# A gated mix of a causal convolution and a spectral filter on one core: chunk 4's products summed on VectorE and POOL, chunk 2's kv unfolded, gate weights loaded apart, halves, and a new order

## The chip, the core and the metric

The kernel runs on one core of a Trainium2 chip. The core has a matrix engine (TensorE, PE in the profile, with PEld for its weight loads), a vector engine (VectorE, DVE), an engine for activations and scaled copies (ScalarE, ACT), a general engine (GpSimd, POOL) and a queue that only issues transfers (SyncE, SP). Matmul results land in PSUM, which this kernel uses as eight banks of 128 x 512 floats; everything else lies in SBUF. POOL reads and writes SBUF only. Transfers are issued from SP and POOL and run on 16 DMA engines.

The metric is the device time of one execution in microseconds, as a median over runs.

## What is computed

Two branches over 2048 positions and 640 channels, mixed by a gate. All data are 32-bit floats.

```python
g = sigmoid((A_q * gate_w).sum(-1, keepdims=True))
# branch A: short causal convolution of k (4 taps), times v, then a causal
# convolution over all 2048 positions, plus a skip term, times q
kv = k_shift * v
y  = irfft(rfft(pad(kv)) * rfft(pad(ssm_k)))[:S] + kv * ssm_D
a  = q * y
# branch B: a two-dimensional real FFT, a product with complex weights, and back
b  = irfft2(rfft2(x) * (w_r + 1j * w_i))          # x is A_q
out = g * a + (1 - g) * b
```

## The kernel before

Both branches are done with Fourier transforms written as matmuls with constant matrices. The length 2048 is split into 64 x 32 and a twist in between; the 640 channels are five chunks of 128. What would be a complex product is four real products, of which pairs are added or subtracted.

Branch B works on one large tile XX. `fwd(u)`, for u from 0 to 7, loads a piece of the transposed input (`xT`), makes four sums and differences of 640 elements on VectorE or POOL (two of a first stage, two of a second) and transforms over the channels (L309, and L316 for the remaining rows) with the matrix `df`. Four columns of `df` hold the gate's weights, so that the gate's sums fall out of the same matmuls; `gate_cols` computes these columns from `gwx`, which lies behind `df` in the same load. `b1(u)` does the first step over the positions (ten times), `bs2(i)` the second and the product with the spectral weights (eight times, with two products and a sum for each of the real and imaginary parts), `i1(u)` the first step back (six times). `bu(n)` is the last step over the positions (16 times), and `dic(v)` the transform back over channels, for v from 0 to 7: matmuls (L447, L453), four scaled copies on ACT (L461), two sums (L465), two more sums (L467), and the store of the rows.

Branch A works chunk by chunk (c from 0 to 4) on one of three slots of a tile YY. `kv(u)`, two for each chunk, does the short convolution as matmuls (L486), the product with v on VectorE (L489), a sum and a difference of the halves, the fold (L495), and a transpose (L498). `hf(u)` loads the long filter. `s1` is the first transform (L530, twice as many matmuls where kv was not folded) and two transposes out of PSUM (L540). `s2(c, m)`, four steps for each chunk, is the second transform of both kv and filter (L560), a copy of the filter's half to SBUF by ACT (L565) and the two products (L581 and L578). For the chunks in `PESUM` the products are written back into YY, and the inverse transform `is1a` adds and subtracts them by having four groups of matmuls accumulate where it would else have two. For the others the products go to two M buffers, and two sums (L586) on VectorE or POOL write YY. `is1a` transforms (L271) and transposes back out of PSUM (L276). `afin(c, n0)`, two for each chunk, is the last transform (L622) and the product with q and the gate (L628). I number afin 0 to 9 (2c for n0 = 0, 2c + 1 for n0 = 8), is1 likewise by chunk and half.

The two branches meet in the output in memory. For chunks 0 to 2 branch A stores first and the rows of `dic` are added to it by an accumulating transfer from POOL (L471). For chunks 3 and 4 `dic` stores its rows (L474) and `afin` follows: afin 6 and 8 by an accumulating transfer from POOL (L641), afin 7 and 9 (those in `BACK`) by reading the rows back (L637), adding them on VectorE (L638) and storing the sum (L639). These read-backs wait until the stores of the four `dic` of their half have landed.

Each unit of work is recorded as an operation with its engine, and nothing runs in the order of the code: `_emit` goes through the list `ORDER`, the result of a planner, which gives the order in which the operations are issued to the in-order queues of all engines. `ON_DVE` says which of the sums and products that either engine could do lie on VectorE; the others lie on POOL. `SLOTS` gives each buffer its place: there are five V buffers (128 x 1024), three T, four M, two L, two H, one G (for k), and the PSUM banks. Where an operation waits follows from what it reads and writes. With `GATE`, an operation of POOL waits for the last VectorE operation ahead of it in the order that reads its operands from SBUF.

## Time and profile before

| | us |
|---|---|
| median of three runs | 285.04 |
| lowest and highest | 282.61 and 285.54 |
| the profiled execution | 283.68 |
| its span, from first to last instruction | 281.6 |

TensorE's mean granted clock in the profiled execution was 0.984 of full speed.

In the rows of the profile a group of instructions is told by its line, its engine and the tiles that it writes and reads. The rows of fp32 matmuls count two records for each matmul of the code. "Idle before" is the time in which the engine had nothing to do in front of these instructions, with what ended it. The chain is the work that ended last, followed back from the end.

### The profile page before, as it was taken

The numbers are of one execution on the slowest core, as the hardware profiler recorded it, in microseconds if no ns is written. First come the engines' busy times: TensorE is split into PE (matmuls) and PEld (weight loads), VectorE is DVE, ScalarE is ACT, GpSimd is POOL, SyncE is SP. The second block draws the span as 40 slices with busy tenths as digits, with TensorE's granted clock in tenths as the row PEclk, the third lists the DMA queues.
The fourth block names the chain that finished last, engine by engine and source line by source line (L and its number), as shares of the span: only waits on it lengthen the run. The fifth ranks groups of instructions, "written<-read, shape, count | busy, mean of one in ns | idle before, by whom it ended". The sixth has DMA issues, their size and how long they took to land.

```text
span 281.6 us, 10200 instructions
## 1 busy us (share of the span) xinstructions
PE 246.3 (87%) x4562; PEld 144.9 (51%) x4562; DVE 224.1 (80%) x250; ACT 103.6 (37%) x232; POOL 150.1 (53%) x116
## 2 busy tenths in 40 slices
PE   0798789899999999788998988999999999999950
PEld 0674445554334454125445433667776677776450
DVE  3979489759998999999999999896464895664970
ACT  1052404451233333362263030546644374445500
POOL 0047557535005574798989710079888328339420
PEclk9999979999999999999999999999999999999996
DMA  7999979959996255687269963626548538737789
GB/s 277 421 416 346 330 264 420 410 123 365 278 389 230 70 98 199 188 338 254 82 165 352 260 121 99 276 80 231 146 115 139 131 54 149 228 54 97 134 200 211
DMA packets 28251, 61.53 MB, mean 218 GB/s; under 512 B 1712, under 2 KB 18480, under 8 KB 26544
## 3 DMA queue, kind: packets, MB, share of 16 engines
q1 hardware_dynamic: 22512, 51.45, 49.8%
q0 software_dynamic: 5696, 9.44, 21.9%
q8 instruction: 36, 0.59, 0.8%
q14 instruction: 7, 0.06, 0.1%
HBM read 50.39 MB, written 10.49 MB: 216 GB/s over the span
## 4 chain that ended last, share of the span: by engine, by line
PE 64%; DVE 15%; DMA 8%; POOL 5%; issue 4%; SPq 1%; ACT 1%; DVEq 0%; POOLq 0%; ACTq 0%
PE banks L560 11%; PE banks L271 11%; PE banks L356 7%; PE banks L447 7%; PE banks L420 7%; PE banks L530 5%; PE banks L622 5%; DMA XX<-xT 4%; DMA V<-h 4%; DVE YY L540 3%; DVE XX L276 3%; PE banks L309 3%; PE banks L453 2%; PE banks L486 2%; PE banks L428 2%
## 5 line engine op out<-in xcount | busy, mean ns | idle before, releaser
L540 DVE STREAM_TRANSPOSE YY<-banks 128x1024 f32<-128x1024 f32 x40 | 48.2, 1227 | 8.4 <-PE banks L530 8.4
L560 PE MATMUL banks<-YY,s2a 64*32 64x256 f32 x1280 | 43.0, 389 | 2.7 <-issue 1.6
L565 ACT ACTIVATE H<-banks 128x512 f32<-128x512 f32 x40 | 23.5, 598 | 39.9 <-PE banks L560 20.2
L495 POOL TENSOR_TENSOR T<-V 128x512 f32<-128x512 f32 x12 | 15.8, 1330 | 41.8 <-DVE V L489 22.0
L560 PEld LDWEIGHTS banks<-YY,s2a 64*32 64x32 f32 x1280 | 24.0, 105 | 19.7 <-issue 6.7
L271 PE MATMUL banks<-YY,ca 32*64 32x512 f32 x512 | 31.1, 607 | 0.6 <-DVE YY L540 0.4
L309 PE MATMUL banks<-cc,XX 128*64 128x162 f32 (+1 forms) x256 | 22.1, 330 | 8.7 <-DVE cc L287 8.7
L612 ACT ACTIVATE V<-V,g 128x128 f32<-128x128 f32 x72 | 21.9, 394 | 14.4 <-DMA V<-q 14.4
L309 PEld LDWEIGHTS banks<-cc,XX 128*64 128x64 f32 x256 | 19.4, 150 | 14.2 <-DVE cc L287 8.7
L581 DVE TENSOR_TENSOR YY<-banks,H 128x512 f32<-128x512 f32 x24 | 16.3, 682 | 13.1 <-ACT H L565 12.8
L276 DVE STREAM_TRANSPOSE YY<-banks 128x2048 f32<-128x2048 f32 x10 | 23.1, 2313 | 3.3 <-PE banks L271 2.9
L303 POOL TENSOR_TENSOR XX<-M 128x640 f32<-128x640 f32 x8 | 12.4, 1557 | 19.3 <-DVE XX L303 13.7
L461 ACT ACTIVATE M<-banks,om 128x320 f32<-128x320 f32 x32 | 14.2, 528 | 21.9 <-PE banks L453 16.2
L395 POOL TENSOR_TENSOR XX<-M,M 128x642 f32<-128x642 f32 x15 | 19.7, 1328 | 4.1 <-DVE M L389 3.4
L271 PEld LDWEIGHTS banks<-YY,ca 32*64 32x64 f32 x512 | 13.3, 129 | 15.5 <-issue 10.6
L356 PE MATMUL banks<-XX,cb 128*128 128x512 f32 (+1 forms) x42 | 20.9, 632 | 0.0
L622 PEld LDWEIGHTS banks<-YY,is2a 128*64 128x64 f32 x320 | 18.1, 134 | 5.3 <-DVE YY L540 1.9
L622 PE MATMUL banks<-YY,is2a 128*64 128x128 f32 x320 | 20.3, 279 | 0.5 <-DVE YY L276 0.5
L447 PEld LDWEIGHTS banks<-di,L 128*128 128x128 f32 x128 | 17.6, 190 | 5.5 <-ACT L L436 3.0
L586 POOL TENSOR_TENSOR YY<-M,M 128x512 f32<-128x512 f32 x14 | 18.5, 1355 | 3.4 <-DVE M L578 1.1
L420 PE MATMUL banks<-cc,XX 128*128 128x128 f32 x128 | 19.4, 295 | 0.4 <-DVE M L578 0.4
L447 PE MATMUL banks<-di,L 128*128 128x160 f32 x128 | 19.5, 306 | 0.0
(70 smaller groups left out, 417.3 us busy)
## 6 DMA issues: line engine op xcount, KB each, us to landing
G<-k SPq DMA_DIRECT2D x10, 1024.0 KB, 8.3
L<-w SPq DMA_DIRECT2D x8, 642.0 KB, 4.7
XX<-xT SPq DMA_DIRECT2D x8, 640.0 KB, 8.7
V<-v SPq DMA_DIRECT2D x10, 512.0 KB, 6.7
V<-h SPq DMA_DIRECT2D x10, 512.0 KB, 9.0
V<-h POOLq DMA_DIRECT2D x10, 512.0 KB, 8.0
V<-q SPq DMA_DIRECT2D x10, 512.0 KB, 5.6
out_dram<-V SPq DMA_DIRECT2D x8, 512.0 KB, 4.6
```

The lines of the kernel that those rows point to most:

```text
L271: mm(p[h * 64:h * 64 + 64, j, :nd * 8], is1[r, sg, ri, :], v[r, h * 2 + src, :, d0:d0 + nd, :].rearrange("p m d e -> p d m e"), start=(i = ...
L276: nc.vector.transpose(by_col(x, d0, nd), p[:, :, :nd * 8].rearrange("p j (d i) -> p d j i", i=8))
L309: mm(bk(p, g_)[ri * 64:ri * 64 + 64, o:o + n], X[:, s, g_ * 64:g_ * 64 + 64], df[:, 0, ri * 323 + o:ri * 323 + o + n], start=(o == 0), sto ...
L356: mm(v(x)[:, e0:e0 + ne], m1b, by_col(XX, d0 + a + e0, ne), start=True, stop=True)
L395: ttop(642, lambda f, ri=ri, o=o, dst=dst: f(dst(), T(t1)[:, ri], T(t2)[:, 1 - ri], op=o), us=1.28, r=[t1, t2, ("t", i, 0, ri), ("t", i, 1 ...
L420: mm(psa[:, t, :, b, :], row(XX, n2)[:, t * 161:t * 161 + 128], W(n2), start=True, stop=True)
L447: mm(bk(p, b)[:, n * 160:n * 160 + 160], U[:, t_, r_], di[:, b * 160:b * 160 + 160], start=(n == 0), stop=False)
L540: op("DVE", dve(1024), lambda b=b: nc.vector.transpose(by_col(YY[:, :, y], a * 64 + b * 32, 32), view(b)), r=[p[b]], w=yk)
L560: mm(ps(p)[j * 32:j * 32 + 32, h].rearrange("p (y r d) -> p y r d", y=2, r=2)[:, :, ri], s2a[r, k, ri * 32:ri * 32 + 32], YY[r, k // 2, y0 ...
L565: op("ACT", act_us(512), lambda p=p, hs=hs: act(sb(hs, 2, 256), ps(p)[:, :, 256:], AF.Copy), r=[p], w=[hs])
L612: act(dst(j), src(j), AF.Copy, scale=g[:, n0 + j:n0 + j + 1])
L622: mm(v()[b * 64:b * 64 + 64, j, :], is2a[:, n2, :], row(YY[:, :, yp], n2), start=True, stop=True)
```

## The change

The diff does these things:

- `PESUM` loses chunk 4. Its products go to two buffers of the pool T (`TP`), two sums for each of the four steps write YY, and its two `is1a` have two groups of matmuls for four.
- `PEFOLD` gains chunk 2: its kv is not folded ahead of the first transform, which has twice as many matmuls there.
- `gwx`, the gate's weights, is loaded into a tile of its own, ahead of `df`, which is now loaded without the four gate columns (in four pieces of 321 columns for each partition). The columns' writers are declared independent of that load.
- The second stage of sums in `fwd` marks each of its halves, and the matmuls are two operations, of which each waits for its half.
- The last adds of afin 7 and 9 and their stores are done in two halves of 512 elements.
- `ON_DVE`, `ORDER` and `SLOTS` are new. Among the things that change place: `fwd(2)` is first where `fwd(0)` was, `fwd(7)` comes behind chunk 0's inverse transforms, afin 4 and 5 stand ahead of `i1`, and is1 7 and afin 6 stand next to the last `dic`, afin 6 behind it.

```diff
 BACK={7,9}
-PESUM={0,2,4}
-PEFOLD=set()
+PESUM={0,2}
+PEFOLD={2}
+TP={4:'T'}
...
+    def apart(these, those):
+
+        for i in these:
+            for j in those:
+                tc.declare_no_dep(i.ins, j.ins.name, reason="the gate's columns are not among the loaded ones")
+
+    def load_df():
+        loaded.append(dma(cc[:, 2048:3340].rearrange("p (b c) -> p b c", c=323)[:, :, 1:322], I["df"].rearrange("p (b c) -> p b c", c=321)))
+        apart(loaded, cols)
+        return loaded[0]
...
-        op("DVE", 0.9, f, w=DF).port = (0, 1)
+        op("DVE", 0.75, f, r=["gwx"], w=["gcol"]).port = (0, 1)
...
-            ttop(640, lambda f, o=o: f(X[:, (2 if o == OP.subtract else 0):][:, :2], Y()[:, 0::2], Y()[:, 1::2], op=o), r=[y], w=[x])
-        blk = ((0, 0, 0, 162), (3, 1, 0, 162), (2, 0, 162, 161), (1, 1, 162, 161))
+            ttop(640, lambda f, o=o: f(X[:, (2 if o == OP.subtract else 0):][:, :2], Y()[:, 0::2], Y()[:, 1::2], op=o),
+                 r=[y, x], w=[("xs", u, int(o == OP.subtract))])
+        blk = ((0, 0, 0, 162), (1, 1, 162, 161), (2, 0, 162, 161), (3, 1, 0, 162))
...
-        op("PE", 2.2, pe, r=[x] + DF, w=p, mode="128x64")
+        for h in range(2):
+            op("PE", 1.1, lambda h=h: pe(h), r=[("xs", u, h), "gcol"] + DF, w=p, mode="128x64")
...
-        t = [] if pesum else [new("M"), new("M")]
+        t = [] if pesum else [new(TP.get(c, "M")), new(TP.get(c, "M"))]
...
-            ttop(1024, lambda f: f(sb(qt, 1024), sb(qt, 1024), sb(bt, 1024), op=OP.add), r=[bt], w=[qt])
-            op("SP", ISS, lambda: dma(out[:, n0:n0 + 8, cs], Q()), r=[qt, bt], kb=524)
+            for h in range(2):
+                hs = slice(h * 512, h * 512 + 512)
+                ttop(512, lambda f, hs=hs: f(sb(qt, 1024)[:, hs], sb(qt, 1024)[:, hs], sb(bt, 1024)[:, hs], op=OP.add), r=[bt, qt], w=[("qh", c, n0, h)])
+                op("SP", ISS, lambda h=h: dma(out[:, n0 + h * 4:n0 + h * 4 + 4, cs], Q()[:, h * 4:h * 4 + 4]), r=[qt, bt, ("qh", c, n0, h)], kb=262)
...
-    op("SP", ISS, lambda: dma(cc[:, 2048:3348], I["df"]), w=DF, kb=666)
+    op("SP", ISS, load_df, w=DF, kb=666)
+    unit("gwx")
+    op("SP", ISS, lambda: dma(gwx, I["gwx"].rearrange("p (a s) -> p a s", a=2)), w=["gwx"], kb=8)
```

The ends of the two orders, by engine, read from the lists (dic 7 is the last transform of the rows; "st1" and "st2" are its first and second pair of sums):

| engine | before | after |
|---|---|---|
| TensorE | bu 14, bu 15, s2 of chunk 4, dic 7, is1 8, is1 9, afin 7, 8, 9 | s2 of chunk 4, bu 14, bu 15, is1 7, dic 7, afin 6, is1 9, is1 8, afin 7, 8, 9 |
| VectorE | products of chunk 4, st1, st1, one st2 of dic 7, transposes of is1 8 and 9, products of afin 7, 8, 9, two adds | products of chunk 4, transpose of is1 7, a sum of chunk 4, product of afin 6, st1, st1 of dic 7, transposes of is1 9 and 8, products of afin 7, 8, 9, four half adds |
| POOL | four sums of dic 6, its accumulating transfer, one st2 of dic 7, its transfer, that of afin 8 | four sums of dic 6, a sum of chunk 4, the transfers of dic 6 and afin 6, both st2 of dic 7, its transfer, that of afin 8 |

29 lines of the change are left out of this document (15 added, 14 removed), and 93 rows, old and new, of tables (ON_DVE, ORDER, SLOTS).

## The prediction

> **What bounds the kernel now.** I read the page first (busy shares, the slices, the shares of the chain that ended last), then the busy time by stretches of 10 us, then the chain in order of time for its end, and the timeline where the chain leaves TensorE.
>
> ```profile
> PE 246.3 (87%) x4562; PEld 144.9 (51%) x4562; DVE 224.1 (80%) x250; ACT 103.6 (37%) x232; POOL 150.1 (53%) x116
> PE   0798789899999999788998988999999999999950
> DVE  3979489759998999999999999896464895664970
> POOL 0047557535005574798989710079888328339420
> PE 64%; DVE 15%; DMA 8%; POOL 5%; issue 4%; SPq 1%; ACT 1%; DVEq 0%; POOLq 0%; ACTq 0%
> ```
>
> ```profile
> 0.00:10.00 10.00, 1.35 (x10) 1.35 (x12) 5.01 (x11) 1.28 (x1) 0.20 (x4) 1.00 0.83 323
> ...
> 20.00:30.00 10.00, 7.99 (x190) 4.42 (x187) 8.35 (x9) 4.11 (x11) 7.58 (x7) 1.00 1.04 354
> 30.00:40.00 10.00, 7.72 (x146) 3.64 (x147) 6.15 (x8) 1.71 (x4) 5.16 (x4) 0.87 0.91 323
> ...
> 110.00:120.00 10.00, 7.77 (x160) 2.25 (x156) 10.00 (x12) 4.62 (x13) 5.99 (x4) 1.00 0.63 194
> 120.00:130.00 10.00, 8.13 (x160) 3.41 (x154) 9.91 (x9) 5.04 (x16) 9.53 (x8) 1.00 0.93 342
> ...
> 240.00:250.00 10.00, 10.00 (x213) 7.57 (x212) 5.47 (x10) 4.61 (x9) 4.31 (x3) 1.00 0.73 189
> ```
>
> Columns: stretch, length, then PE, PEld, DVE, ACT and POOL busy, granted clock, DMA share, GB/s. There are four regimes. Up to 10 us TensorE waits for its first input. From 20 to 40 the DMA share is 0.91 to 1.04 and TensorE is idle 2.01 + 2.28 us. From 110 to 130 VectorE is full (10.00, 9.91) and TensorE is not (7.77, 8.13). From 200 on TensorE is full (the row at 240) and VectorE half idle. Then the end:
>
> ```profile
> 257.14 0.76 PE banks L453 x16
> 257.90 7.37 PE banks L271 x126
> 265.29 2.33 DVE YY L276
> 267.67 3.93 PE banks L622 x56
> 272.76 1.23 DVE V L638
> 274.00 1.23 DVE V L638
> ```
>
> I call the end of the last transform of the rows (L453, at 257.90) the cut. After it come 7.37 us for chunk 4's two inverse groups of four parts, a transpose, 3.93 for two final products, one multiplication and two adds. A second path leaves the same cut:
>
> ```profile
> 258.02 1.78 ACT L461 ACTIVATE M<-banks,om 128x320 f32<-128x320 f32 x4 [2.54 <-PE banks L453]
> 259.89 1.68 DVE L465 TENSOR_TENSOR M<-M 128x640 f32<-128x640 f32 x2 [2.50 <-POOL M L467]
> 262.53 1.56 POOL L467 TENSOR_TENSOR M<-M 128x640 f32<-128x640 f32 x1 [1.89 <-DVE M L467]
> 266.42 1.37 SPq L637 DMA_DIRECT2D V<-out_dram  x2
> 271.54 1.56 POOL L641 DMA_DIRECT2D out_dram<-V  x1 [5.95 <-issue]
> 274.04 2.02 SPq L639 DMA_DIRECT2D out_dram<-V  x2
> V<-out_dram SPq DMA_DIRECT2D x2, 512.0 KB, 6.5
> out_dram<-V SPq DMA_DIRECT2D x2, 512.0 KB, 5.2
> out_dram<-M SPq DMA_DIRECT2D x2, 256.0 KB, 2.2
> ```
>
> The last rows (dic 7) are scaled, added twice and stored, the store lands, and only then are the rows read back that L638 adds. POOL ends at 264.09, the read-backs start at 266.42 and take 6.5 us: 272.9. The path through TensorE reaches its first add at 272.76. **The two paths arrive together**, so shortening one of them alone gives nothing at the end.
>
> **The change, part by part.** I numbered the operations in the order in which the code creates them and read both order lists with that.
>
> ```profile
> L540 DVE STREAM_TRANSPOSE YY<-banks 128x1024 f32<-128x1024 f32 x40 | 48.2, 1227 | 8.4 <-PE banks L530 8.4
> L586 POOL TENSOR_TENSOR YY<-M,M 128x512 f32<-128x512 f32 x14 | 18.5, 1355 | 3.4 <-DVE M L578 1.1 <-ACT M L461 0.9 <-DVE V L511 0.8
> L495 POOL TENSOR_TENSOR T<-V 128x512 f32<-128x512 f32 x12 | 15.8, 1330 | 41.8 <-DVE V L489 22.0 <-PE banks L560 18.1 <-PE banks L530 1.7
> 231.43 1.08 PE banks L530 x32
> 251.29 1.15 PE banks L420 x8
> 252.43 0.36 PE banks L428 x16
> 252.79 1.98 PE banks L560 x58
> 254.77 2.37 PE banks L447 x16
> ```
>
> *Products of chunk 4 not summed on PE.* The two inverse groups go from four parts to two: -7.37/2 = -3.7 us of TensorE, all after the cut. Added are eight sums, four on each of POOL (4 x 1.355 = 5.4 us) and VectorE. They use two T buffers a step, and steps share them, so a step's first product on VectorE now waits for the sums of the step before, and VectorE's later work queues behind it.
>
> *kv of chunk 2 unfolded.* Four folds go (three from POOL, 3 x 1.33 = 4.0 us, one from VectorE) and two first transforms double: +2 x 1.08 = +2.2 us of TensorE.
>
> *Work moved past the cut.* The first final product of chunk 3 (3.93/2 = 1.97 us) now stands behind the cut. TensorE's work before the cut is therefore +2.2 - 2.0, and since the order puts nothing else across it, **+0.2 us**: none of the 3.7 us is saved before the cut.
>
> *After the cut, counted from it.* Before, the first add comes at 272.76 - 257.90 = 14.9 and the span's end at 281.6 - 257.9 = 23.7. In the new order TensorE does afin 6 from 0 to 2.0, is1 9 to 3.9 and is1 8 to 5.7 (1.85 each); VectorE has the multiplication of afin 6 to 3.3 (it waits for TensorE's 2.0), dic 7's two sums to 4.9 (1.68), then two transposes of 2.33 to 9.6. Chunk 4's final products wait for the second and end at 13.5, the last multiplication at 14.7: so of 3.7 us on TensorE only 0.2 come through, since VectorE's queue is late next. The other path: dic 7's last sums are both on POOL (before, one was on VectorE): 4.9 + 2 x 1.56 = 8.0, then 2.3 until the read-backs start as before (264.09 to 266.42): 10.3, and 6.5 to land: 16.8. This path is now 1.9 us later than before. Four half adds of 1.23/2 end at 19.3, not 17.3. Against that, the store is of 256 KB: it takes between 2.2 us (the rows' own store, alone) and 5.2 (the 512 KB store in its crowd). I take 3.2, nearer the small one, since chunk 4's accumulating store (afin 8, from POOL at 12.7) has a lead on the last store of 6.6 us (before, 3.8: 271.5 to 275.3): 19.3 + 0.1 + 3.2 = 22.6, and the 1.1 us between the last landing (275.3 + 5.2 = 280.5) and the span's end make 23.7, as before. I write **0** for the end. The bounds are -3.1 (the read-backs hidden, so that the first add starts at 14.7 and not 16.8, and a store of 2.2 and not 3.2) and +3.2 (below).
>
> *The start.*
>
> ```profile
> 4.89 1.56 DVE L301 TENSOR_TENSOR M<-XX 128x640 f32<-128x640 f32 x2 [4.89 <-DMA XX<-xT]
> 8.51 0.16 DVE L288 TENSOR_TENSOR cc<-gt 128x4 f32<-128x4 f32 x1
> 8.65 4.64 PE L309 MATMUL banks<-cc,XX 128*64 128x162 f32 x32 [8.65 <-DVE cc L287]
> 36.47 1.49 PE L530 MATMUL banks<-V,ca 32*32 32x512 f32 x32 [2.27 <-DVE V L511]
> 42.59 0.69 PE L560 MATMUL banks<-YY,s2a 64*32 64x256 f32 x16
> ```
>
> TensorE starts at 8.65, behind four sums (4.89 to 8.0) and the gate's columns. With the first transform in halves it needs three sums and the columns, which stand second on VectorE: 7.9, so -0.7. The small load of the gate's weights is one more issue (about 0.4 us) ahead of the matrix, hidden behind the 4.89 us that xT takes; uncovered it costs that 0.4. The order also puts one more half transform and its remainder, 1.9 us of TensorE, ahead of the first filter product at 42.59, which otherwise has the same work before it (five whole first transforms and the matmuls of a sixth, three convolutions, four first transforms of chunk 0). One more xT lands ahead: 640 KB at the 323 to 354 GB/s of the rows from 20 to 40 are 1.9 us, and the filter's constants were issued long enough before 42.59 to bear that. If the wait at 36.47 is filled as the list says, the start and this stretch together give **-1.9**; the bounds are 0 and -4.3 (all of the 2.01 + 2.28 idle).
>
> *The middle.* Ahead of the first inverse transform of the spectral half (i1), the new order does 13.6 us more TensorE work (two final products 3.9, four first transforms and two doubled halves 6 x 1.08, two filter products 2.0, one convolution) and 13.7 more on VectorE (eight transposes of 1.227, two multiplications, kv 9, three first sums, less some), but only 1.6 more on POOL, since folds and first sums left it. Both engines' work goes up alike in a stretch where both were nearly full, so i1 starts about 13.6 later and 13.5 less is left behind it: **0**, with bounds of -4.1 (all of TensorE's idle in the rows at 110 and 120, 2.23 + 1.87) and +3.7 (VectorE idles in the added 13.6 us as it does from 20 to 40: 1.65 + 3.85 in 20).
>
> Sum: start and early stretch -1.9, TensorE before the cut +0.2, middle 0, end 0: -1.7. The profiled execution took 283.68 (span 281.6, 2.1 around it), so 282.0 by its own time. The median of the three runs is 285.04, 0.5% above it; against that median I forecast **283.3**.
>
> **The rivals.**
>
> *POOL holds the end back (slower).*
>
> ```profile
> L465 POOL TENSOR_TENSOR M<-M x8: 1547/1560/2197, 201.8 to 253.6; 128x640 f32<-128x640 f32 x8
> ```
>
> One of POOL's sums of 640 took 2.2 us in place of 1.56, beside VectorE's work. In the new order POOL has four sums of dic 6 and one of chunk 4 in front of is1 9, and 12 such operations from chunk 4's first product on, each of whose T buffers stops VectorE. At 0.64 more apiece: five ahead of is1 9 make 3.2 us at the end; the other seven, through T buffers and PSUM, up to 4.5: +7.7 in all, 283.3 + 7.7 = 291.0. It makes the kernel slower by over 1% from 4.6 us on, about 0.38 apiece. Against it: the median of that row is 1560 and the sums' row L586 has a mean of 1355. The Trainium skill (GPSIMD Engine Reference, Specifications) says that POOL's way to SBUF is shared with VectorE and that VectorE's instructions with two SBUF inputs contend with it. By that rule the sums of dic 6 and dic 7 would be met, and it speaks against moving chunk 4's sums off TensorE; the trace shows it in one of eight.
>
> *The middle loosens (faster).* POOL was busy 9.53 us of 10 at 120 beside a full VectorE, and TensorE idle 1.87. If folds and sums that left POOL free VectorE's waits there, the middle gives its -4.1: 279.2; with half of the end's bound in addition 277.7. For it: the rows at 110 and 120. Against it: VectorE itself is full there and its own work is not less.
>
> *Nothing is seen.* The early waits are set by the bytes (share 1.04), the same bytes come, and the end has two paths that arrive together: 285.0.
>
> **How the numbers follow.** Forecast 0.42 (281.7 to 284.7), middle loosens 0.28 (277.7 to 281.7), nothing seen 0.14 (284.7 to 286.5), POOL holds 0.16 (286.5 to 291.0). A measurement of this kernel can tell about 1%, 2.85 us, from no change: faster is below 282.2, slower above 287.9. Faster: all of the loosened middle, 0.28, and 0.12 of the forecast, whose lower part lies below 282.2: 0.40. Slower: 0.14 of POOL's 0.16, and 0.02 for an order whose added waits lie elsewhere: 0.16. Same: 0.44. The range leaves out the lowest 0.08 and the highest 0.12: 278.7 to 288.0.
>
> **What would show it.** The first matmul at 7.9 and not 8.65. The first filter product still near 42.6 with fwd of six and a half units before it. The last L453 about 2 us earlier than 257.9. After it, 3.7 us (not 7.37) in L271, but VectorE's transposes ending near 9.6 and the read-backs starting near 10.3 after the cut, so that the end still lies about 23.7 behind it. POOL's 640 sums staying at 1.56. The forecast is wrong if POOL's sums stretch, if TensorE idles over 2 us more between 170 and the cut (T buffers), or if VectorE's full stretch ends earlier than its added work says.

## The result: slower by about 1%

| | us |
|---|---|
| changed kernel, median of four runs | 287.6 |
| its lowest and highest | 285.89 and 288.75 |
| kernel before, measured with it | 285.0 |
| ratio, with its 95% interval | 1.0115 (1.0075 to 1.0155) |
| profiled execution of the changed kernel, and its span | 285.89 and 284.1 |

The forecast of 283.3 had the wrong sign. Its range (278.7 to 288.0) holds the median. The profiled execution is the fastest of the four. Its span of 284.1 against the 281.6 of before, **2.5 us**, is what can be read from the two traces, and it is about as much as the medians are apart (287.6 - 285.0). Medians here and below are of all executions of a kernel, while ratios and their intervals leave out executions in a slower state, so a ratio isn't always that of the two medians.

### The profile page after: what moved, and what is told of

It reads as the page before. It is cut to its first block, busy times and chain, and to the rows that moved or that the text cites. A ratio compares the mean times of both kernels' runs of the same rounds, so it can differ in the third digit from the quotient of the medians.

```text
span 284.1 us, 10225 instructions
## 1 busy us (share of the span) xinstructions
PE 244.1 (86%) x4562; PEld 144.7 (51%) x4562; DVE 228.3 (80%) x252; ACT 105.1 (37%) x234; POOL 154.7 (54%) x120
## 3 DMA queue, kind: packets, MB, share of 16 engines
q0 software_dynamic: 5696, 9.44, 21.4%
## 4 chain that ended last, share of the span: by engine, by line
PE 58%; DVE 21%; DMA 10%; issue 5%; SPq 2%; POOL 1%; ACT 0%; DVEq 0%
PE banks L578 10%; PE banks L272 9%; PE banks L465 7%; PE banks L374 6%; PE banks L438 6%; DVE YY L558 5%; PE banks L548 5%; DMA V<-v 4%; PE banks L640 4%; DMA V<-h 4%; DVE YY L277 3%; DMA V<-out_dram 2%; PE banks L396 2%; PE banks L471 2%; DVE XX L277 2%
## 5 line engine op out<-in xcount | busy, mean ns | idle before, releaser
L558 DVE STREAM_TRANSPOSE YY<-banks 128x1024 f32<-128x1024 f32 x40 | 47.6, 1224 | 8.6 <-PE banks L548 8.5
L578 PE MATMUL banks<-YY,s2a 64*32 64x256 f32 x1280 | 43.9, 388 | 0.7 <-DVE YY L596 0.4
L578 PEld LDWEIGHTS banks<-YY,s2a 64*32 64x32 f32 x1280 | 23.4, 105 | 19.1 <-issue 4.8
L326 PE MATMUL banks<-cc,XX 128*64 128x161 f32 (+1 forms) x256 | 22.0, 324 | 9.9 <-DMA cc<-df 9.1
L272 PE MATMUL banks<-YY,ca 32*64 32x512 f32 x448 | 27.7, 608 | 2.2 <-DVE YY L277 1.1
L604 POOL TENSOR_TENSOR YY<-M,M 128x512 f32<-128x512 f32 x16 | 20.6, 1320 | 12.0 <-DVE M L596 6.0
L326 PEld LDWEIGHTS banks<-cc,XX 128*64 128x64 f32 x256 | 18.6, 147 | 16.5 <-DVE XX L319 9.5
L479 ACT ACTIVATE M<-banks,om 128x320 f32<-128x320 f32 x32 | 14.6, 527 | 21.9 <-PE banks L471 17.4
L319 POOL TENSOR_TENSOR XX<-M 128x640 f32<-128x640 f32 x7 | 11.1, 1596 | 20.6 <-DVE XX L319 17.8
L413 POOL TENSOR_TENSOR XX<-M,M 128x642 f32<-128x642 f32 x16 | 21.3, 1345 | 0.4 <-DVE T L513 0.3
L465 PEld LDWEIGHTS banks<-di,L 128*128 128x128 f32 x128 | 17.6, 190 | 4.4 <-issue 2.7
L485 POOL TENSOR_TENSOR M<-M 128x640 f32<-128x640 f32 x10 | 15.8, 1578 | 6.9 <-DVE M L485 6.4
L465 PE MATMUL banks<-di,L 128*128 128x160 f32 x128 | 19.5, 306 | 0.0
L438 PEld LDWEIGHTS banks<-cc,XX 128*128 128x128 f32 x128 | 16.4, 197 | 4.4 <-issue 1.6
```

The costliest lines, as they stand in the source:

```text
L272: mm(p[h * 64:h * 64 + 64, j, :nd * 8], is1[r, sg, ri, :], v[r, h * 2 + src, :, d0:d0 + nd, :].rearrange("p m d e -> p d m e"), start=(i = ...
L326: mm(bk(p, g_)[ri * 64:ri * 64 + 64, o:o + n], X[:, s, g_ * 64:g_ * 64 + 64], df[:, 0, ri * 323 + o:ri * 323 + o + n], start=(h == 0), sto ...
L413: ttop(642, lambda f, ri=ri, o=o, dst=dst: f(dst(), T(t1)[:, ri], T(t2)[:, 1 - ri], op=o), us=1.28, r=[t1, t2, ("t", i, 0, ri), ("t", i, 1 ...
L438: mm(psa[:, t, :, b, :], row(XX, n2)[:, t * 161:t * 161 + 128], W(n2), start=True, stop=True)
L465: mm(bk(p, b)[:, n * 160:n * 160 + 160], U[:, t_, r_], di[:, b * 160:b * 160 + 160], start=(n == 0), stop=False)
L558: op("DVE", dve(1024), lambda b=b: nc.vector.transpose(by_col(YY[:, :, y], a * 64 + b * 32, 32), view(b)), r=[p[b]], w=yk)
```

## The profile after

First the page's busy times of the changed kernel.

```profile
PE 244.1 (86%) x4562; PEld 144.7 (51%) x4562; DVE 228.3 (80%) x252; ACT 105.1 (37%) x234; POOL 154.7 (54%) x120
```

TensorE has 2.2 us less than the 246.3 of before, VectorE 4.2 more than 224.1, POOL 4.6 more than 150.1. To see where this matters, the span is cut at the same three events in both kernels: the first filter product, the first block-row transform (`bu`), and the cut, with the end as a fourth row. Columns: stretch, length, then PE, PEld, DVE, ACT and POOL busy, granted clock, DMA share, GB/s. Before:

```profile
0.00:42.60 42.60, 29.58 (x530) 19.59 (x530) 30.60 (x40) 10.21 (x23) 17.17 (x16) 0.96 0.93 343
42.60:175.00 132.40, 121.09 (x2308) 56.26 (x2306) 122.66 (x133) 45.31 (x101) 76.23 (x59) 1.00 0.72 232
175.00:257.90 82.90, 82.46 (x1524) 60.84 (x1515) 57.86 (x69) 41.59 (x88) 49.94 (x37) 1.00 0.60 147
257.90:281.60 23.70, 13.18 (x224) 8.23 (x224) 12.94 (x10) 6.45 (x20) 6.76 (x5) 0.89 0.83 170
```

and after:

```profile
0.00:43.50 43.50, 30.43 (x576) 20.25 (x576) 33.62 (x42) 11.78 (x27) 16.05 (x15) 1.00 0.97 353
43.50:190.30 146.80, 133.51 (x2612) 63.73 (x2611) 136.67 (x146) 51.60 (x118) 80.49 (x63) 1.00 0.77 245
190.30:258.80 68.50, 68.50 (x1194) 52.01 (x1188) 43.94 (x54) 35.24 (x69) 48.08 (x35) 1.00 0.42 83
258.80:284.10 25.30, 11.66 (x192) 8.71 (x192) 14.10 (x13) 6.45 (x20) 10.03 (x8) 0.84 0.93 178
```

Subtracting the rows: TensorE's work ahead of the cut changes by 0.85 + 12.42 - 13.96 = -0.69. Its idle time ahead of the cut (length less busy) goes from 13.02 + 11.31 + 0.44 to 13.07 + 13.29 + 0: +1.59, of which **1.98 arise in the second stretch**. So the cut comes 0.9 later, and the end is 25.3 - 23.7 = **1.6** longer. That is the 2.5.

One part of this belongs to the execution. The kernel with an eighth of one transfer (under "The end" below) has the same order and differs only in the size of an accumulating transfer at the end. In its profile the first filter product is at 42.67 and not 43.5, and the cut at 257.90, as before the change: TensorE's idle time up to the first filter product is 0.7 less than before, its work up to the cut 0.8 less, and its idle time from there to the cut again 1.5 more. Its end is again 25.3 long. So the middle and the end lose the same in both profiles, 1.5 and 1.6, and the 0.9 at the cut belongs to the early part of one execution.

The first stretch begins with this (timeline, changed kernel):

```profile
1.66 0.66 SPq L290 DMA_DIRECT2D cc<-df  x1
6.84 1.56 DVE L319 TENSOR_TENSOR XX<-M 128x640 f32<-128x640 f32 x2
9.07 4.34 PE L326 MATMUL banks<-cc,XX 128*64 128x162 f32 x32 [9.07 <-DMA cc<-df]
```

VectorE's sums are done at 8.40 and the gate's columns before that, but `df` lands at 9.07, 7.4 us after its issue. That is the latest of twelve profiles with this start (the changed kernel and those made from it): their first matmul comes at 7.91 to 9.07, in five of them by 8.04.

In the second stretch, the worst part is this (busy time in four windows, same columns, and their sum with the fifth window 170 to 174):

```profile
154.00:158.00 4.00, 1.58 (x48) 0.24 (x32) 4.00 (x4) 1.38 (x2) 3.92 (x4) 1.00 0.49 173
158.00:162.00 4.00, 2.52 (x64) 0.81 (x64) 3.95 (x6) 1.93 (x6) 3.92 (x4) 1.00 0.56 163
162.00:166.00 4.00, 3.22 (x78) 1.51 (x80) 4.00 (x6) 3.64 (x13) 4.00 (x4) 1.00 0.86 318
166.00:170.00 4.00, 4.00 (x82) 3.01 (x80) 4.00 (x5) 1.23 (x2) 4.00 (x4) 1.00 1.00 320
...
sum 20.00, PE 15.22 PEld 7.10 DVE 19.95 ACT 8.77 POOL 19.84; mean PE 3.04 PEld 1.42 DVE 3.99 ACT 1.75 POOL 3.97
```

In these 20 us VectorE (19.95) and POOL (19.84) are both full, and TensorE is busy 15.22. Its waits there end with VectorE's transposes (2.2 + 1.4 + 1.2 us in the view of waits); none is put down to POOL.

The end (the first two lines from the chain, the last from the view of transfers, the others from the timeline of the changed kernel):

```profile
258.02 0.76 PE banks L471 x16
263.52 4.52 DVE YY L277 x2
260.85 3.82 PE L272 MATMUL banks<-YY,ca 32*64 32x512 f32 x64
263.69 3.42 POOL L485 TENSOR_TENSOR M<-M 128x640 f32<-128x640 f32 x2
269.80 1.37 SPq L655 DMA_DIRECT2D V<-out_dram  x2
275.62 1.29 DVE L658 TENSOR_TENSOR V<-V,V 128x512 f32<-128x512 f32 x2 [2.36 <-DMA V<-out_dram]
277.15 1.29 DVE L658 TENSOR_TENSOR V<-V,V 128x512 f32<-128x512 f32 x2 [0.23 <-DMA V<-out_dram]
out_dram<-V SPq DMA_DIRECT2D x4, 256.0 KB, 4.3
```

Chunk 4's two inverse transforms take 3.82 us and not 7.37, and it is worth nothing: the adds wait for the read-backs. These start 11.0 after the cut (before, 8.5), since both last sums of dic 7 stand on POOL until 267.11. The last add ends 19.64 after the cut (277.15 + 1.29 - 258.80), and the span 5.66 after that: the half stores take 4.3 us (median of the four).

## The experiments

The kernel before was measured again beside each group of runs; ratios are against it.

**The order alone, and the parts alone.** The first kernel has the new order and none of the parts; the folds of chunk 2's kv, which the new order does not have, stand on POOL right ahead of their transposes. The second has the old order with all parts except chunk 4's; in it the product of chunk 2's kv is overwritten before its transpose has read it, so that chunk 2 of its output is another.

```diff
 order_alone: ORDER, SLOTS, ON_DVE of the changed kernel; PESUM={0,2,4}, PEFOLD=set()
 parts_alone: ORDER, SLOTS, ON_DVE of the kernel before; PESUM={0,2,4}, PEFOLD={2}
```

> The new order with every part of the change undone (chunk 4 summed by TensorE, chunk 2 folded, df and gwx in one load with the gate's columns behind the first four sums, first transform in one operation, whole last adds and stores). Theory O, the loss lies in the order (VectorE's full stretch is longer and its instructions are stretched beside POOL's; the last rows' path to the read-backs is longer): 286 to 288 us, as the changed kernel or a little less. Rival P, the loss lies in the parts (sums of chunk 4 through shared T buffers, doubled transforms, df in pieces, four stores): 285 or less.

> The order of before with the parts that fit into it: chunk 2 unfolded, gwx apart and df in pieces, first transform in halves, last adds and stores in halves; chunk 4 stays summed by TensorE, since its steps are interleaved there and three T buffers would not do. Theory O: 283 to 285.5, no loss (TensorE +2.2 us for the doubled transforms in a stretch where VectorE is full, the halves of the last store give up to 1 us). Rival P: 286 or more.

Measured: the order alone 296.02, 1.0453 (1.0406 to 1.0499); the parts alone 289.46, 1.0191 (1.015 to 1.0232). Both theories were missed: the order alone lost far more than it said, and for the parts the rival's 286 or more came true. The order alone is clearly worse than the whole change; the parts alone are hardly to be told from it (the intervals touch). In the order alone, TensorE is idle in the second stretch 157.30 - 135.94 = 21.4 us (windows), 8 more than in the changed kernel, and the timeline of POOL shows a part of why: a pair of folds waits 6.40 us for the product on VectorE, and two of VectorE's transposes behind such folds wait 2.7 us each. The rest was not taken apart, and it may hang on the place that the folds were given here.

```profile
sum 157.30, PE 135.94 PEld 65.30 DVE 138.25 ACT 51.83 POOL 85.48; mean PE 45.31 PEld 21.77 DVE 46.08 ACT 17.27 POOL 28.49
92.81 2.49 POOL L495 TENSOR_TENSOR T<-V 128x512 f32<-128x512 f32 x2 [6.40 <-DVE V L489]
```

**Chunk 4's products back on TensorE**, in the changed kernel.

```diff
-PESUM={0,2}
+PESUM={0,2,4}
```

> The changed kernel with chunk 4's products summed by TensorE again: eight sums less on VectorE and POOL, 3.7 us more of TensorE after the last row transform. If the read-backs of the last rows set the end (first add 16.85 us after the last row transform), TensorE's path of 14.7 + 3.7 = 18.4, less the VectorE wait of some 1.5 that it fills, arrives with them: within 1 us of the changed kernel's 287.6. Rival, TensorE's time counts in full at the end: 291.

Measured 287.66, 1.0157 (1.0109 to 1.0204), where the changed kernel has 1.0115 (1.0075 to 1.0155): no difference that the intervals can tell. 3.7 us of TensorE at the end, with the eight sums that replace them, are worth nothing that can be seen, much as the prediction had it (0.2).

**The start alone, the unfolding alone, the last halves alone**, each in the kernel before and its order. In the second, the transpose of kv 4 stands somewhat earlier, and its result is overwritten before the transform has read it, so that chunk 2 of the output is another.

```diff
 start_alone:       df without the gate's columns, gwx loaded apart, first transform's matmuls in halves
 unfold_alone:      PEFOLD={2}
 last_halves_alone: for h in range(2): the add of 512 elements and its store
```

> The kernel before, with its own order, and of the change only the start: the transform's constants loaded without the gate's columns (four pieces of 321 columns for each partition), the gate's weights by a load of their own, and the first transform's big part issued in halves. Theory (the start is a loss, not the gain of 0.75 us that the prediction took): the load of df in pieces lands about 7.4 us after its issue where the whole one took 5.2, the first matmul starts at 9.0 to 9.6 and not at 8.65, and the later start is carried to the end: 285.0 to 286.0 us against 284.2 to 285.0 of the kernel before. Rival (the prediction's step was right, and the late df in the changed kernel came from the new order of loads): first matmul at 7.9, time 283.5 to 284.2.

> The kernel before, with its own order, and of the change only that kv of chunk 2 isn't folded: four sums less on VectorE and POOL, each of the two transforms 32 matmuls longer; the transpose of the first of the two stands a little earlier in the order. Theory (the unfolding pays only in an order that has TensorE idle at that place; in the old order it is TensorE time of about 3.6 us in a stretch where TensorE is nearly full): 286.5 to 288.5 us, the cut 2 to 3.5 us later than 257.9. Rival (the four sums were what held VectorE and POOL, so that the loss of the parts in the old order came from elsewhere): 283 to 285 us.

> The kernel before, and of the change only the last two additions and stores in halves. Everything up to the last additions stays; the first half-store is issued 0.6 us sooner after its addition. Theory: 283.5 to 284.8 us, a gain of 0.3 to 0.8 at most, because the four half-stores share the same queue rows as the two whole ones (4.3 us median in the changed kernel against 3.2 for a whole one before). Rival (the halves cost by their own issues, four of 0.6 us on one queue): 285.0 to 286.0 us.

Measured: the start 1.0005 (0.9974 to 1.0036), the unfolding 1.0162 (1.0105 to 1.022), the halves 1.0014 (0.9985 to 1.0042). The theory of the start was half right. It gains nothing, but no loss is seen at the end either (the interval is about 0.9 us each way). The unfolding cost more than its theory's 286.5 to 288.5: its cut is at 263.71, 5.8 later than before. The halves missed their gain of 0.3 to 0.8; in their expectation the whole store before is given 3.2 us, while the trace has 5.2, and the halves took 4.4. The start's timeline:

```profile
7.58 0.17 DVE L298 TENSOR_SCALAR gwx<-gwx 128x8 f32<-128x8 f32 x1 [1.28 <-DMA gwx<-gwx]
9.08 3.23 PE L326 MATMUL banks<-cc,XX 128*64 128x162 f32 x22 [9.08 <-DVE XX L319]
```

The load of 4 KB, issued at 1.90, lands at 7.58; the gate's columns wait for it, the second sums stand behind them, and TensorE starts at 9.08. So the halves that gained nothing and the start that gained nothing leave the order and the unfolding. They belong together. With chunk 4 summed on TensorE throughout, the ratio with folded kv is 1 (old order) and 1.0453 (new), with unfolded kv 1.0162 (old) and 1.0157 (new, with the start and the halves). The old order is hurt by the unfolding, and the new one, with the folds where this experiment put them, needs it.

**Which engine bounds the second stretch.** Two kernels take the same time from one engine each, a third moves VectorE work behind the first inverse. In this third one, a transform of chunk 4 is written over the results of two block-row transforms before they are copied out, so that parts of the output are others.

```diff
 dve_less: -tt(dst(), Z(), W(), op=OP.mult)
           +tt(dst()[:, :, :nw], Z()[:, :, :nw], W()[:, :, :nw], op=OP.mult)   # nw = 1 for ri = 0 of bs2 0 to 4
 pe_less:  +parts = parts[:2] if c == 2 else parts
 first_inverse_sooner: s1Y 8 behind bu 3; bs2(2)'s first sum on VectorE; h 8's transfer behind its second
```

> The changed kernel; five of the filter step's sixteen VectorE products (0.79 to 0.83 us each, between 123 and 170 us) are made on 2 columns in place of 642, the rest of these five products is left out. That takes about 3.5 us from VectorE and nothing from TensorE. Theory (in the new order VectorE bounds the stretch from the first filter product to the last back-transpose of the first inverse: 13.9 us more VectorE work were put into it and 12.3 us more TensorE work): the first block-row transform and the cut come 2.5 to 3.5 us sooner, the time is 284.0 to 285.2 against 287.4. Rival (TensorE's own order, or the loads, bound it): less than 1 us.

> The changed kernel; the two inverse transforms of chunk 2 (near 145 to 153 us) add up two of their four parts, the other two are left out of the result. That takes about 3.7 us from TensorE in the same stretch and nothing from VectorE. Theory (VectorE bounds it): the cut moves by less than 1 us, time 286.7 to 287.6. Rival (TensorE's work, the unfolded transforms among it, bounds it): 3 us or more, 284 to 284.6.

> The changed kernel with the work ahead of the first inverse thinned in one place, nothing left out: one transform of chunk 4 with its two VectorE transposes (2.46 us) goes behind the first inverse, the last filter sum on POOL (1.33) goes to VectorE beside the other one, POOL's accumulating load of h comes after both, and one product pair gets other banks, so that the first inverse can start at about 173.2 and not at 175.25. Theory (VectorE's work ahead of the first inverse is the bound): the last back-transpose ends 1.3 to 2 us sooner, and the time is 285.7 to 286.3. Rival (what is put off is missing later, behind the first inverse, where TensorE waits for nothing): 287 to 288.

Measured: 287.91, 1.0111 (1.0048 to 1.0174); 288.97, 1.0101 (1.0021 to 1.018); 295.58, 1.0418 (1.0358 to 1.0478). The theory that VectorE alone bounds the stretch fell. The kernel with less VectorE work, its second stretch and a piece of its chain:

```profile
42.10:189.00 146.90, 133.28 (x2612) 65.02 (x2610) 133.93 (x147) 51.61 (x118) 80.57 (x63) 1.00 0.78 248
149.17 1.34 POOL M L407
151.53 1.57 POOL M L407
153.18 1.34 POOL XX L414
```

VectorE has 2.74 us less in it, and the stretch is as long as in the changed kernel (146.9 and 146.8). Where that kernel's chain ran through TensorE and VectorE, it now runs in this piece through POOL's products and sums. That POOL is the second limit is read from this; no run took work from VectorE and POOL at once. With less TensorE work the time is the same too, but its profile has a fall of the clock in this stretch (last section), so the run decides little. In the third kernel the first block-row transform comes 150.1 us after the first filter product and not 146.8, and the cut 73.3 after that and not 68.5. What holds it was not looked for, and it says nothing on the question.

**TensorE kept busy in that stretch.** 22 matmuls into columns of a bank that nobody reads, in the changed kernel and in the version with the re-ordered end (below).

```diff
+for i, n in enumerate((7, 8, 7)):
+    for _ in range(n):
+        mm(banks[:, 1, 328:488], cons["is2a"][:, :128], cons["is2a"][:, :160], start=True, stop=True)
```

> The changed kernel with 22 matmuls added (each 128 x 128 weights by 160 columns, about 0.15 us, into columns of a bank that nobody reads), in three groups of about 1.1 us, at the three places between 154 and 162 us where TensorE waits for VectorE's transposes. Nothing else changes, the output is the same. Theory (the new order leaves TensorE so idle at 154 to 158 that in a part of the executions its granted clock falls to 0.50 from 158 to 162 and from 166 to 170, which costs them 2.5 to 3 us; the fillers keep it busy): the granted clock stays at 1.00 there, no execution lies at 288 or above, the mean clocks are 0.984 or more and the median is 285.5 to 286.3. Rival (the falling clock has another cause, and the added matmuls only delay the work behind them): 287.5 to 289.5, mean clocks from 0.965 to 0.985 as before.

> The version with the re-ordered end and blocks 6 and 8 read back early (285.26 us in its run), with the same three groups of added matmuls. Theory: its executions above 286 go, median 284.2 to 285.0, within 0.3% of the kernel before. Rival: 285.5 to 287.

Measured: 294.23, 1.034 (1.03 to 1.0381), and 293.39, 1.0299 (1.0243 to 1.0355). Both lie above their rivals, too. The added matmuls didn't do what they were made for. The first group's row, and the second stretch:

```profile
156.35 2.17 PE L692 MATMUL banks<-is2a 128*128 128x160 f32 x14 [2.66 <-ACT M L406]
42.70:196.30 153.60, 140.17 (x2656) 70.62 (x2654) 136.90 (x146) 51.63 (x118) 80.71 (x63) 1.00 0.74 236
```

Each of the 22 took 0.3 us, twice what the expectation gave, and the first group waited 2.66 us for ACT's copy (L406) out of the bank that it writes, and so stood in the way of the real matmuls. 6.7 us of TensorE work (140.17 against 133.51) lengthened the stretch by 6.8, and TensorE is still idle 13.4 us in it (13.3 without). So the work went behind the waits and not into them; the run doesn't show what work that fitted into the waits would cost. With the kernel that has less VectorE work, the reading is that TensorE, VectorE and POOL hand each other the banks and sums in turn, so that less on one link is taken up by another. It fits the two runs, and is argued, not shown.

**The turns taken away**, in the kernel before.

```diff
-GATE = True
+GATE = False
```

> The kernel before, without the waits by which a POOL sum stands behind the VectorE operation on SBUF operands ahead of it: order, engines and work are the same, POOL may run beside VectorE anywhere. Measures the price of the overlap. Theory (a VectorE sum that falls beside a POOL sum loses up to 1.2 us and POOL loses nothing, and VectorE bounds the stretch ahead of the last first-inverse transpose): VectorE's longest 640-element sum goes from 0.83 to 1.9 us or more, its busy time grows by 3 us or more from 224.1, and the time by 1 to 3 us: 286 to 288 us. Rival (what VectorE loses, POOL's earlier start gives back): VectorE busy grows as much, and the time stays within 0.7 us of the kernel before.

Measured 296.88, 1.032 (1.0254 to 1.0385): far more than the theory's 286 to 288, and against the rival. VectorE's and POOL's groups, first of the kernel before, then without the turns:

```profile
L495 DVE TENSOR_TENSOR T<-V 128x512 f32<-128x512 f32 x8 | 5.5, 703 | 0.1
L301 DVE TENSOR_TENSOR M<-XX 128x640 f32<-128x640 f32 x9 | 7.2, 818 | 4.9 <-DMA XX<-xT 4.9
```

```profile
L495 DVE TENSOR_TENSOR T<-V 128x512 f32<-128x512 f32 x8 | 11.0, 1385 | 0.1
L301 DVE TENSOR_TENSOR M<-XX 128x640 f32<-128x640 f32 x9 | 9.9, 1120 | 4.8 <-DMA XX<-xT 4.8
L465 POOL TENSOR_TENSOR M<-M 128x640 f32<-128x640 f32 x8 | 13.6, 1700 | 1.9 <-ACT M L461 1.3 <-issue 0.3
```

Without the turns VectorE's sums of 512 take 1385 ns and not 703, in the mean of eight. POOL loses less: its sums of L465 take 1700 and not 1682, those of L301 1810 and not 1552. The changed kernel has a little of it, in spite of the turns:

```profile
L317 DVE TENSOR_TENSOR M<-XX 128x640 f32<-128x640 f32 x11 | 9.8, 925 | 6.8 <-DMA XX<-xT 6.8
L513 DVE TENSOR_TENSOR T<-V 128x512 f32<-128x512 f32 x6 | 4.9, 842 | 0.1
```

that is 11 x (925 - 818) + 6 x (842 - 703) = 2.0 us more on VectorE.

**The end.** Six kernels. In the first three, the changed kernel's last part: dic 7's sums first; the same with chunk 4's last POOL sum ahead of them and a T buffer for one read-back; and only an eighth of afin 6's accumulating transfer.

```diff
 last_rows_first:    dic 7's s0, s1, s2 on VectorE ahead of afin 6's product
 tail2:              s2(18)'s second sum ahead of them; dic 7's s2 on POOL, s3 on VectorE; bt = new("V" if c == 4 else "T")
 after_block6_eighth: nb = 1 if c == 3 else 8;  out[:, n0:n0 + nb, cs], Q()[:, :nb]
```

> The changed kernel with the last rows' four sums in front: both first sums and one second sum of dic 7 on VectorE ahead of afin 6's product, the other second sum on POOL ahead of the accumulating transfers of dic 6 and afin 6, its store at once. The read-backs start some 3.4 us earlier (7.6 after the last row transform, not 11.0), TensorE's path takes over at about 15.3: the end comes 1.5 to 2 us earlier, 285.6 to 286.1. Rival, the end is set by something else (the stores' own traffic): no change from 287.6.

> The changed kernel, with its end re-ordered: the last rows' first two sums go ahead of the product of the sixth output block on VectorE, the third goes to POOL and the fourth to VectorE right behind that product; chunk 4's last POOL sum stays ahead of all of them; and one of the two read-backs gets a buffer that no accumulating transfer holds. Theory (the end is set by the chain last rows' sums, store, read-backs, additions, stores): the store is issued at about 264.6 and not 267.1, the read-backs at about 267.0 and not 269.80, and the end comes 2.3 to 2.9 us sooner: 284.7 to 285.4 us. Rival A (the read-backs wait for the sixth block's accumulating transfer as well, and the transposes that now start 1 us later hold the last products): 286.5 to 287.6. Rival B (the end is set by the transfers' share of the DMA engines after 262, whatever their order): within 0.5 us of 287.6.

> The changed kernel; of the sixth output block's accumulating transfer only an eighth is made (64 KB in place of 512 KB; the rest of this block is left out of the output). Nothing else changes. Theory (this transfer, which stood ahead of the cut before and now starts 3.5 us behind it, fills the DMA engines in which the read-backs and the last stores run, and holds the buffer of one read-back): the read-backs land 1 to 2 us sooner, the last stores take about 3.3 us and not 4.3, and the time is 285.0 to 286.3 against 287.3 to 287.6 of the changed kernel. Rival (the end hangs on the time at which the last rows are summed, 267.1, whatever else is under way): 287.0 to 287.6.

Measured: 293.04, 1.0333 (1.0295 to 1.037); 287.27, 1.0109 (1.0057 to 1.0161); 288.08, 1.0125 (1.009 to 1.016). All three theories missed. The first has an end of 31.4 us after its cut, and made two new waits: chunk 4's last sum on POOL had to take its turn behind dic 7's, and one read-back, which has afin 6's slot, came behind afin 6's late transfer.

```profile
266.43 1.27 POOL L605 TENSOR_TENSOR YY<-T,T 128x512 f32<-128x512 f32 x1 [4.59 <-DVE M L486]
272.65 11.15 SPq L656 DMA_DIRECT2D V<-out_dram  x2
```

The second took both away, and the read-backs started at 268.41 and not 269.80 (9.6 after the cut and not 11.0), but took 7.9 and 9.7 us and not 6.3 (the view of transfers), beside afin 6's accumulating transfer, now issued at 266.20:

```profile
268.41 0.38 SPq L656 DMA_DIRECT2D V<-out_dram  x1
V<-out_dram SPq DMA_DIRECT2D x1, 512.0 KB, 7.9
T<-out_dram SPq DMA_DIRECT2D x1, 512.0 KB, 9.7
out_dram<-V POOLq DMA_DIRECT2D x2, 512.0 KB, 8.8
```

In the third, where that transfer is small but dic 7's sums are late as in the changed kernel, the read-backs take 6.9 us, and the end is as long (25.3). So the end seems to ask for two things at once: early sums of dic 7, and no accumulating transfer beside the read-backs. The other three test that. Block 8 (in the kernel before) or blocks 6 and 8 (in the changed one) are read back early, added on POOL and stored plainly; in the last, block 6's stores stand behind the read-backs in SP's queue.

```diff
-BACK={7,9}
+BACK={6,7,8,9}          # {7,8,9} in the kernel before
-bt = new("V")
+bt = new({6: "G", 7: "T", 8: "T", 9: "V"}[2 * c + n0 // 8])
```

> The kernel before, with block 8's accumulating transfer replaced by an early read-back (its rows are stored long before), an addition on POOL right behind its product, and a plain store by SP. Theory (the DMA engines are the bound of the end): the transfer issued at 271.54, 7 us long and twice as dear as a plain store, goes, the last two stores take 2.3 to 2.8 us and not 3.2: 283.5 to 284.5 against 284.9. Rival (the addition on POOL and the third store by SP stand in the way of the last two): 285.2 to 286.5.

> The changed kernel with the re-ordered end of the earlier run (last rows' sums first) and with both the sixth and the eighth output block read back early, added on POOL and stored plainly, so that no 512 KB accumulating transfer is left behind the cut. Theory (the end is bound by the DMA engines from 266 to 280, and the two accumulating transfers are its dearest part): the read-backs take about 6 us or less and not 7.9 and 9.7, the last addition ends by 276.5 and not 279.8, the time is 283.5 to 285.5. Rival (the read-backs and stores alone fill the engines): 286.5 to 287.5.

> As the earlier run with blocks 6 and 8 read back early, but block 6's two stores stand behind the two last read-backs in SP's queue and not ahead of them. Theory (what held that run was the read-backs' place in SP's queue behind stores that waited for POOL: they were issued 10.9 us after the cut, though the last rows' store had been issued 6.5 after it): read-backs 8.8 to 9.2 us after the cut, the last addition 18 to 18.7 after it, the end 22.8 to 23.5 after it and not 25.3; time 284.5 to 285.8. Rival (the read-backs are slowed by what goes beside them, as in the run with the last rows' sums first, by as much as they come sooner): 286.5 to 287.5.

Measured: 284.21, 1.0000 (0.9971 to 1.0029); 286.69, 1.0088 (1.0059 to 1.0116); 285.26, **1.0049 (1.0013 to 1.0084)**. In the kernel before, block 8's transfer costs nothing. In the changed one the profiled execution of the first version has a fall of the clock ahead of the cut (last section) and an end of 24.2; in the last, both together give the length that the prediction thought the end would have (its timeline):

```profile
257.63 0.83 PE L472 MATMUL banks<-di,L 32*128 32x160 f32 x16
267.97 0.38 SPq L656 DMA_DIRECT2D V<-out_dram  x1
276.27 1.28 DVE L659 TENSOR_TENSOR V<-V,T 128x512 f32<-128x512 f32 x2
```

Its cut is at 258.46, the read-backs start 9.5 after it, the last add ends 19.1 after it and the span 23.6 (282.1 - 258.46): the 1.6 us of the end are gone, and with them about half of the loss (1.0049 against 1.0115). No version was faster than the kernel before.

## Why the prediction was wrong, step by step

In us against the kernel before; the last column is the other profile of the same order, with an eighth of afin 6's transfer.

| step | predicted | changed kernel | the other profile |
|---|---|---|---|
| start and early stretch (TensorE's idle time) | -1.9 | +0.05 | -0.7 |
| TensorE's work before the cut | +0.2 | -0.7 | -0.8 |
| the middle (TensorE's idle time from the first filter product to the cut) | 0 | +1.5 | +1.5 |
| the end | 0 | +1.6 | +1.6 |
| sum | -1.7 | +2.5 | +1.6 |

**The start failed, as a step.** The prediction took the new load of `df` to be as long as the old one and the gate's load to be hidden behind xT. `df`, in four pieces for each partition, lands 5.9 to 7.4 us after its issue in the twelve profiles with this start, against 4.9 to 5.2 whole, and the first matmul comes at 7.91 to 9.07: as predicted (7.9) in the best of them, and at 9.07 in the changed kernel's own profile. In the kernel with the start alone it is the gate's load of 4 KB that takes 5.7 us. It was named as a price of 0.4 if uncovered; it was more. What failed in both columns is the early stretch: of the 1.9 us of idle time that were to go, at most 0.7 went. The long wait of 2.27 us that ended at 36.47 is gone, but six shorter ones of 0.2 to 1.0 us stand in the new order between 20 and 43 us, where before there were two besides it. The first filter product is at 43.52 and 42.67, not ahead of where it was.

**The middle failed, as a step.** Its reason was that both engines' work ahead of the first inverse of the spectral half (i1) goes up alike, 13.6 and 13.7, so that i1 starts 13.6 later and nothing is lost. i1 starts at 159.53 before and at 175.25 after, 15.7 later. Up to there, before and after:

```profile
0.00:159.53 159.53, 137.73 (x2578) 71.53 (x2586) 138.05 (x163) 52.55 (x115) 91.80 (x74) 0.99 0.80 273
0.00:175.25 175.25, 150.24 (x2914) 78.87 (x2915) 155.48 (x177) 60.33 (x136) 93.97 (x76) 1.00 0.83 277
```

TensorE has 12.5 us more, VectorE 17.4 and POOL 2.2 (predicted 1.6). So the equality on which the step rested was not there: VectorE's term was too small by 3.7. Some 2.0 of VectorE's are sums stretched beside POOL's, a cost that the prediction gave to POOL in a rival and to VectorE nowhere. But VectorE isn't the whole cause, since 2.74 us less on it changed nothing; from 154 to 174 POOL is as full as VectorE. The upper bound of +3.7 held what was lost, 1.5. The prediction's sign of being wrong here was VectorE's full stretch ending earlier than its added work says; the added work was larger than it says, and i1 came later.

**The end was right in its mechanism and mis-sized in a term.** Predicted and measured, after the cut: read-backs 10.3 and 11.0, first add 16.8 and 16.8, last add 19.3 and 19.64. Chunk 4's 3.7 us came to nothing, nearly as said, and the experiment that undid it agrees. The term that was off is the last store: 3.2 us for 256 KB, measured 4.3, with afin 8's transfer and the other half stores under way beside it (that these slow it is likely, but was not tested by itself). From the last add to the end it is 5.66 and not 4.4. The halves alone, which the prediction counted on to make up for the late read-backs, are worth nothing (1.0014). What the prediction didn't see is that the late place of afin 6, behind the cut, puts its transfer among the read-backs as soon as dic 7's sums are made earlier (the runs took it away together with afin 8's).

**The rivals.** "POOL holds the end back" had the right sign, for another reason. POOL's sums of 640 hardly stretched (median 1.55 us, longest 2.00; before, one of 2.20); it was VectorE's that did. By the rule of the Trainium skill that the prediction cited (GPSIMD Engine Reference, Specifications), the two contend. The traces agree, and in the changed kernel VectorE loses more: sums of 640 with a median of 0.82 us took up to 1.98. "The middle loosens" spoke for the opposite of what happened: POOL had 2.2 us more to do ahead of i1, not less. "Nothing is seen" is what three of the parts give: the start and the last halves by themselves, and chunk 4 where it was taken back.

**What stays open.** The cause of the middle's 1.5 us. Which of TensorE, VectorE and POOL would have to be relieved, alone or together, and by how much, was not found. The other profile's loss is 1.6 and not the 2.6 of the medians, and that kernel's other executions (286.89 to 288.49 against 285.01) were not taken apart either.

## What to carry to other kernels

Where two engines are full and a third waits for them by turns, "all grow alike" is no estimate of zero: count each engine's work in that stretch, POOL's and stretched sums too, and don't take the idle time of the third for a reserve untested. Look at a second profile of the same order before a late start is put down to the change. Parts of a change that were planned together may each be worth nothing or a loss alone; try an order with and without the part that it was made for before judging either. At the end of a kernel, ask of each transfer what runs beside it: an earlier read-back gained nothing until the accumulating transfer beside it was gone.

## What the runs showed of the hardware

**Falls of the granted clock.** Two of the kernels above, the two with blocks 6 and 8 read back early, have the same order up to the last part, but their cuts lie at 261.38 and 258.46. Busy time in three windows of the first (the eighth number is the granted clock), then of the second:

```profile
156.00:158.00 2.00, 0.55 (x24) 0.15 (x16) 2.00 (x3) 1.38 (x2) 2.00 (x2) 1.00 0.75 267
158.00:160.00 2.00, 2.00 (x46) 0.59 (x49) 1.75 (x2) 0.08 (x1) 1.92 (x3) 0.57 0.60 231
166.00:168.00 2.00, 2.00 (x30) 0.74 (x16) 1.59 (x3) 0.43 (x1) 0.71 (x1) 0.50 1.01 397
```

```profile
156.00:158.00 2.00, 0.56 (x32) 0.07 (x15) 2.00 (x3) 1.38 (x2) 2.00 (x2) 1.00 0.88 295
158.00:160.00 2.00, 2.00 (x64) 0.74 (x64) 2.00 (x3) 0.18 (x1) 1.96 (x2) 1.00 0.67 238
166.00:168.00 2.00, 2.00 (x50) 1.24 (x46) 2.00 (x4) 0.27 (x1) 2.00 (x3) 1.00 1.02 363
```

In both, TensorE was busy 0.85 us from 154 to 156 and about 0.55 from 156 to 158; then its clock fell to a half in the one execution and not in the other, and the cut came 2.9 us later. The Trainium skill (TensorE: Matmul & The Clock Gate, What's actually happening) says that the clock is halved after an idle window of some 3.4 us, and that the window runs freely. The values of one half and full speed agree, and so does that the same instructions meet it in one execution only. But TensorE was not idle for 3.4 us at a stretch here; its longest wait from 154 to 158 was 1.45.

The kernel with less TensorE work there shows such a fall too, and so does the one with dic 7's sums first. A fall need not cost anything: the kernel before has one in its own profile (0.50 from 37.5 to 40.5, after the wait of 2.27 us), and the kernel with the last halves alone, the same up to the cut, has none and its cut no earlier, at 258.24 against 257.90. In the changed kernel's own profile there is none ahead of the cut. Its executions reach from 285.89 to 288.75, but those of the kernel before are spread as widely (282.61 to 285.54). The mean clocks of its slower executions, 0.979 to 0.981 against 0.985, point to lost clock in them, but not to where; that it was such a fall is argued, not shown.

**Transfers.** A store of half the size wasn't half as long: in the kernel before, the last stores took 5.2 us as two of 512 KB and 4.4 as four of 256 KB. A load of 4 KB among the large ones at the start took 5.7 and 6.2 us to land in the two kernels where it was issued behind `df`, and 3.5 to 3.9 ahead of it. `df` took 4.9 to 5.2 us as it was (six profiles) and 5.9 to 7.4 in four pieces for each partition (fourteen).
